# A planner that prices transfers by their packets, and a last tile whose sums lie in two places of PSUM

## The chip, the cores and the metric

The kernel runs on one core of a Trainium2 chip. The metric is device time in microseconds (us) of one execution. TensorE is called PE, its weight load PEld, VectorE DVE, ScalarE ACT, GpSimd POOL and SyncE SP. A q behind an engine's name (SPq, ACTq) is its sequencer, which issues DMAs.

## What is computed

Block-causal attention over 8 batches of 8 heads (576 positions of width 64), and behind it a gated feed-forward layer over the 4608 tokens, all in float32:

```python
scores = scale * np.matmul(q, k.transpose(0, 1, 3, 2))
mask = block_i >= block_j                    # blocks of 64 positions
scores = np.where(mask, scores, -1000000000.0)
attn = np.exp(scores - np.max(scores, axis=-1, keepdims=True))
attn = attn / (np.sum(attn, axis=-1, keepdims=True) + 1e-09)
x = np.matmul(attn, v)                       # (tokens, 512)
g = x @ w_gate                               # 512 x 1536
val = x @ w_val                              # 512 x 1536
out = (g * (1.0 / (1.0 + np.exp(-g))) * val) @ w_out     # 1536 x 512
```

q, k and v are float32; the three weights arrive as float64 words and are made float32 on the chip.

## The kernel before, in words

**Feed-forward.** The 4608 tokens are cut into 18 tiles of 256. A tile walks through the 12 chunks of 128 hidden columns two at a time (`feed_forward`): 24 matmuls against the gate's weights into a PSUM tile `gv` (lines 969 to 971), 24 against the value's weights into the other, then on ACT and DVE the tanh (L1002), two products (L1005, L1010), and the result split into a high and a low part `hhl` (cast L1015 on ACT, subtraction L1018 on DVE). From `hhl` and the weights of the output the down products (L1060 to L1062) go into the sums `po`, a PSUM tile of [128, 2, 512]: two blocks of 128 tokens, m = 0 and 1. Each product is made of three matmuls: high times high, high times low, low times high. After the last pair of chunks the sums are copied to SBUF by ACT (L1080) and stored by SP (L1084), one copy and one store for each m.

**Weights.** There are 36 pieces (12 chunks, of gate, value and output). Each is loaded as 512 KB into one of five slots `wo` (L822), made float32 by two steps of ACT (L837, L841) and two of DVE (L846, L851), and split into high (ACT L856) and low (DVE L859). Parts of the output's weights are written to `wo_d` in HBM (L875, L878) and fetched again by every later tile (L1035).

**Attention.** Batches 0 and 1 are "early": their queries come in stretches of 256 and 320, q and k are loaded in blocks of 96 rows (L359), turned on PE (L383), copied by ACT (L391), multiplied (L409), evacuated (L427, L432, L450, L453), reduced to a maximum (DVE L583, POOL L587), subtracted (DVE L611), put through exp (ACT L615) and multiplied with v (L655, v loaded by L632 and L637). Their PSUM tiles are `at` (two) and, for early batches, also `po`. Later batches load q and k by L482 and multiply at L535.

**What sets the order.** Every operation is a task with an engine, a cost in us, a rank, what it comes after, and the buffers it uses. The function `in_order` plays the engines through time: a free engine takes the ready task of the lowest rank whose buffers have room. For a transfer it keeps one clock, `queue`: the transfer occupies all of it for `t.moves`, and lands 0.9 us later:

```python
if t.moves:
    queue = max(queue, end + 0.65) + t.moves
    done = queue + 0.9
```

The resulting list is the order in which each engine's instructions stand in the program. On the chip each engine works through its own list in order and waits at each instruction for what it needs; there is no second choice. SP's list is nearly all of the DMA issues, and a transfer also waits for the one that used the same of eight semaphores, eight transfers earlier.

In `dma` (lines 155 to 159) `t.moves` is the size over 360 KB per us, whatever the transfer's shape; several calls give a round size (3e5 for a v load or an x store).

Of the kernel before, what the change touches and what calls it, by code (L numbers as in the profile page):

```python
# [18 lines left out]
def kernel(  # L19
# [17 lines left out]
    nc = tc.nc  # L37
    B, H, S, D = q.shape
    NT, DM = out.shape
    DFF = w_gate.shape[1]  # L40
    P = 128
# [4 lines left out]
    SP = NKC * P  # L46
# [11 lines left out]

    FINE = 4

    PATIENCE = 10.0
# [5 lines left out]
    TILES = [XT] * (NT // XT)  # L67
# [74 lines left out]
    def act_us(n):  # L142
        return 0.08 + n * 0.000833
# [10 lines left out]

    def dma(rank, size, fn, after=(), bufs=(), n=1, engine="SP"):

        t = add(engine, 0.5 * n, rank, fn, after, bufs)
        t.moves = size / 3.6e5
        return t
# [121 lines left out]
    for i in range(7):  # L281
        n = 2**i
# [31 lines left out]
    def attention(R, b, h, a, e, early, bufs, lane):  # L314
# [9 lines left out]
        W = e - a  # L324
# [25 lines left out]
        def plain_scores():  # L350
# [4 lines left out]
            def load_qk(i, queue):  # L355
# [9 lines left out]
            ld = [  # L365
                dma(R, 5e4 * len(blocks[1]), lambda: load_qk(0, nc.sync), [], [qk], 2),
                dma(R, 5e4 * len(blocks[1]), lambda: load_qk(1, nc.scalar), [], [qk], 2, "ACT")
                if early and a == b == 0
                else dma(R, 5e4 * len(blocks[1]), lambda: load_qk(1, nc.sync), [], [qk], 2),
            ]  # L370
# [97 lines left out]
        def split_scores():  # L468
# [19 lines left out]
            for i in range(2):  # L488
# [15 lines left out]

                ld = dma(R, 3e5, lambda i=i: load(i), [], [raw], 4)
                tr = add("DVE", dve_us(S), R, turn, [ld], [raw, turned, high, *prt])
# [134 lines left out]

        vl = dma(R, 3e5, load_v, [], [vt], 3 if e % P else 2)
        segs = [s for s in ((0, 2 * P), (2 * P, S)) if a <= s[0] and s[1] <= e]
# [124 lines left out]

        t = dma(R, 3e5, x_out, ends, [xu])
        x_done.extend((b, hd, a + here, e, t) for hd in heads)  # L770
# [21 lines left out]
    def weight(i, kind):  # L792
# [30 lines left out]

        t = chain["w"] = dma(R, 5e5, load, [chain["w"]], [raw])
        bufs = [raw, wo] if wo else [raw]
# [44 lines left out]
        if kind == 2:  # L870
            w_kept[i] = t, wo, part

            def store():
                if wo:
                    nc.sync.dma_start(out=wo_d[i], in_=wo[0].bitcast(F32))  # L875
                    return
                for j in range(2):
                    nc.sync.dma_start(  # L878
                        out=wo_d[i][:, j].rearrange("p (n m) -> p n m", n=parts), in_=part(j).bitcast(F32)
                    )  # L880

            t = dma(R, 5e5, store, [t], [wo] if wo else [], 2 if away else 1)
            if away:
                before_place.append((t, away))
# [59 lines left out]
    def feed_forward(j, t0, w, xs):  # L944

        E = 0.5 + j / 1000.0
        nb = w // P
        acc = Buf("po", also=("at",) if j == 1 else ())
        ends = [None] * nb
# [36 lines left out]
        for i in range(0, NFC, 2):  # L986
# [65 lines left out]
            for piece in pieces:  # L1052

                def products(i=i, piece=piece, hh=hh, took=took):
                    for y, m in piece:
                        whi, wlo = (took[y][2](k) for k in range(2))
                        bs = slice(y * w + m * P, y * w + (m + 1) * P)
                        po = acc[0][:, m].rearrange("p (n m) -> p n m", n=whi.shape[1])
                        hi, lo = hh[0][:, bs], hh[1][:, bs]
# [5 lines left out]
                after = [a, *(took[y][0] for y in ys), *{ends[m] for m in ms}]  # L1065
                bufs = [acc, hh, *(took[y][1] for y in ys if took[y][1])]
                t = add("PE", mm_us(DM, DM, DM) * len(piece), rank(i), products, after, bufs)
# [8 lines left out]
        for m in range(nb):  # L1076
            ob = Buf("ob", "out")

            def out_of_psum(m=m, ob=ob):
                nc.scalar.copy(ob[0], acc[0][:, m])  # L1080

            def store(m=m, ob=ob):
                r0 = t0 + m * P
                nc.sync.dma_start(out=out[r0 : r0 + P, :], in_=ob[0])  # L1084

            e = add("ACT", act_us(DM), E, out_of_psum, [ends[m]], [acc, ob])
            dma(E, 2.6e5, store, [e], [ob])

# [184 lines left out]
```

## Time and profile before

| | |
|---|---|
| three runs | 1189.08, 1189.09, 1189.10 us; median 1189.09 |
| the profiled execution | 1189.82 us |
| its span, first to last instruction | 1188.0 us |
| PE busy | 1152.1 us, 97% of the span |
| DVE, ACT, POOL busy | 760.3, 638.0, 325.7 us |
| DMA | 197.39 MB, 166 GB/s over the span |
| mean granted TensorE clock | 0.996 of full speed |

How to read it: busy time is the union of an engine's instructions. The page has the span in 40 slices, each engine's busy share in tenths. A window's line gives the length of a stretch, then for PE, PEld, DVE, ACT and POOL the busy us and the number of instructions, the mean granted clock, the DMA engines' busy share and GB/s. A line of the timeline is: start, duration, engine, source line, operation, written tile <- read tiles, shape, how many in a row, and in brackets the idle time before it and what ended it. A line of the chain (the work that ended last, followed back) has start, duration and what.

### The profile page before, as it was taken

The numbers are of one execution on the slowest core, as the hardware profiler recorded it, in microseconds if no ns is written. First come the engines' busy times: TensorE is split into PE (matmuls) and PEld (weight loads), VectorE is DVE, ScalarE is ACT, GpSimd is POOL, SyncE is SP. The second block draws the span as 40 slices with busy tenths as digits, with TensorE's granted clock in tenths as the row PEclk, the third lists the DMA queues.
The fourth block names the chain that finished last, engine by engine and source line by source line (L and its number), as shares of the span: only waits on it lengthen the run. The fifth ranks groups of instructions, "written<-read, shape, count | busy, mean of one in ns | idle before, by whom it ended". The sixth has DMA issues, their size and how long they took to land.

```text
span 1188.0 us, 21711 instructions
## 1 busy us (share of the span) xinstructions
PE 1152.1 (97%) x8464; PEld 1030.1 (87%) x8464; DVE 760.3 (64%) x1233; ACT 638.0 (54%) x1150; POOL 325.7 (27%) x138
## 2 busy tenths in 40 slices
PE   6789999999999999999999999999999999999998
PEld 4557777898889899989898989898989899999997
DVE  5889879766678585957686768576767533323222
ACT  5879957756566655556565555474736312212111
POOL 3121211033444433324342525243253400000000
PEclk9899999999999999999999999999999999999999
DMA  7857765675556656665656456555652455444442
GB/s 184 231 160 212 211 176 173 174 216 141 145 159 179 177 145 158 178 194 159 174 168 184 149 155 165 185 147 183 165 179 99 157 162 171 155 169 135 142 133 98
DMA packets 266838, 197.39 MB, mean 166 GB/s; under 512 B 195248, under 2 KB 231104, under 8 KB 266736
## 3 DMA queue, kind: packets, MB, share of 16 engines
q1 hardware_dynamic: 264304, 195.42, 56.5%
q8 instruction: 66, 1.08, 0.4%
q10 hardware_dynamic: 2432, 0.59, 0.2%
q14 instruction: 36, 0.29, 0.1%
HBM read 171.57 MB, written 24.38 MB: 165 GB/s over the span
## 4 chain that ended last, share of the span: by engine, by line
PE 85%; DVE 5%; ACT 5%; DMA 3%; issue 1%; POOL 0%; SPq 0%; ACTq 0%; POOLq 0%
PE gv L969 15%; PE gv L971 15%; PE gv L970 15%; PE po L1060 8%; PE at L655 8%; PE po L1061 8%; PE po L1062 8%; PE at L535 7%; DMA wo<-in_moe_w_gate_dram 1%; DVE sc L611 1%; DMA wo<-in_moe_w_val_dram 1%; PE at L409 1%; ACT ob L837 1%; ACT qk L497 1%; DVE mx L583 1%
## 5 line engine op out<-in xcount | busy, mean ns | idle before, releaser
L587 POOL PARTITION_ALL_REDUCE mx<-mx x80 | 144.7, 1855 | 397.4 <-DVE mx L583 155.8
L971 PE MATMUL gv<-xhl,v_all 128*128 128x256 f32 x864 | 239.6, 277 | 1.9 <-DVE v_all L859 1.9
L969 PE MATMUL gv<-xhl,v_all 128*128 128x256 f32 x864 | 241.1, 279 | 0.2 <-DVE t L1005 0.2
L706 POOL PARTITION_ALL_REDUCE mx<-mx x48 | 178.7, 3770 | 224.1 <-DVE mx L583 192.0
L970 PE MATMUL gv<-xhl,v_all 128*128 128x256 f32 x864 | 239.4, 277 | 0.0
L1005 DVE SCALAR_TENSOR_TENSOR t<-t,gv 128x512 f32<-128x512 f32 x108 | 73.8, 684 | 200.0 <-ACT t L1002 199.7
L969 PEld LDWEIGHTS gv<-xhl,v_all 128*128 128x128 f32 x864 | 162.2, 188 | 3.7 <-issue 1.9
L971 PEld LDWEIGHTS gv<-xhl,v_all 128*128 128x128 f32 x864 | 162.3, 188 | 2.1 <-DVE v_all L859 2.1
L970 PEld LDWEIGHTS gv<-xhl,v_all 128*128 128x128 f32 x864 | 162.3, 188 | 0.9
L1060 PE MATMUL po<-wo,hhl 128*128 128x512 f32 x396 | 157.0, 396 | 1.6 <-ACT ob L1080 1.6
L1061 PE MATMUL po<-wo,hhl 128*128 128x512 f32 x396 | 154.9, 391 | 0.0
L1062 PE MATMUL po<-wo,hhl 128*128 128x512 f32 x396 | 154.4, 390 | 0.0
L1002 ACT ACTIVATE t<-gv 128x512 f32<-128x512 f32 x108 | 64.7, 599 | 158.4 <-PE gv L971 158.0
L1015 ACT CAST hhl<-t 128x512 fp32r<-128x512 f32 x108 | 67.0, 621 | 129.7 <-DVE t L1010 125.2
L611 DVE TENSOR_TENSOR sc<-sc,mx 128x640 f32<-128x640 f32 (+6 forms) x168 | 122.5, 768 | 15.5 <-POOL mx L587 15.2
L1018 DVE TENSOR_TENSOR hhl<-t,hhl 128x512 fp32r<-128x512 f32 x108 | 94.6, 876 | 49.2 <-ACT hhl L1015 48.5
L615 ACT ACTIVATE sc<-sc 128x1024 f32<-128x1024 f32 (+3 forms) x104 | 105.5, 1030 | 37.5 <-DVE sc L611 36.4
L969 PE MATMUL gv<-xhl,g_even 128*128 128x256 f32 x432 | 123.4, 286 | 1.3 <-DVE t L1005 1.2
L971 PE MATMUL gv<-xhl,g_even 128*128 128x256 f32 x432 | 122.2, 283 | 0.2 <-DVE g_even L859 0.2
L970 PE MATMUL gv<-xhl,g_even 128*128 128x256 f32 x432 | 122.1, 283 | 0.0
L969 PE MATMUL gv<-xhl,g_odd 128*128 128x256 f32 x432 | 121.1, 280 | 0.0
L970 PE MATMUL gv<-xhl,g_odd 128*128 128x256 f32 x432 | 119.6, 277 | 0.0
(154 smaller groups left out, 2411.6 us busy)
## 6 DMA issues: line engine op xcount, KB each, us to landing
wo<-wo_d SPq DMA_DIRECT2D x200, 512.0 KB
out_dram<-ob SPq DMA_DIRECT2D x36, 256.0 KB
v<-in_v_dram SPq DMA_DIRECT2D x64, 128.0 KB
xt<-x_d SPq DMA_DIRECT2D x64, 128.0 KB
rt<-r_d SPq DMA_DIRECT2D x128, 64.0 KB
qk<-in_q_dram SPq DMA_DIRECT2D x112, 72.0 KB
qk<-in_k_dram SPq DMA_DIRECT2D x104, 72.0 KB
x_d<-xu SPq DMA_DIRECT2D x24, 288.0 KB
```

Of the source, the lines that this page charges most:

```text
L587: nc.gpsimd.partition_all_reduce(m, m, channels=P, reduce_op=bass_isa.ReduceOp.max)
L611: nc.vector.tensor_tensor(piece(c), scores_of(c), m, ALU.subtract)
L615: nc.scalar.activation(x, x, AF.Exp)
L655: nc.tensor.matmul(ps[0][own(x), 1 - i if sums else i, q0 - s0 : s1 - s0], lhsT=ones if sums else vt[0][:, 2 * lane + c, own(x)], rhs=sc[0 ...
L706: nc.gpsimd.partition_all_reduce(m, m, channels=P, reduce_op=bass_isa.ReduceOp.add)
L969: nc.tensor.matmul(o, lhsT=hi[:, d], rhs=xhi[:, 0:w], start=first, stop=False)
L970: nc.tensor.matmul(o, lhsT=hi[:, d], rhs=xlo[:, 0:w], start=False, stop=False)
L971: nc.tensor.matmul(o, lhsT=lo[:, d], rhs=xhi[:, 0:w], start=False, stop=last)
L1018: nc.vector.tensor_tensor(hh[1][:, 0:n], t[0][:, 0:n], hh[0][:, 0:n].bitcast(F32), ALU.subtract)
L1060: nc.tensor.matmul(po, lhsT=hi, rhs=whi, start=i + y == 0, stop=False)
L1061: nc.tensor.matmul(po, lhsT=hi, rhs=wlo, start=False, stop=False)
L1062: nc.tensor.matmul(po, lhsT=lo, rhs=whi, start=False, stop=i + y == NFC - 1)
```

## The change

Three things are changed. The planner's transfers get a length from their packet size (the contiguous bytes of one piece): a packet of n bytes takes 9 + 0.0385 n ns on one of 16 DMA engines. So a megabyte takes 2.95 us in the planner's eyes at 1024 bytes (the default), 4.60 at 256, 6.80 at 128 and 2.54 at 4096, where it was 2.78 for all. The sizes of some loads are put right at the same time (v, x, the first q blocks). `AHEAD` is empty and `LATER` is 0.0, so what they are put into is unchanged.

```diff
-    def dma(rank, size, fn, after=(), bufs=(), n=1, engine="SP"):
+    def dma(rank, size, fn, after=(), bufs=(), n=1, engine="SP", packet=1024):
 
         t = add(engine, 0.5 * n, rank, fn, after, bufs)
-        t.moves = size / 3.6e5
+        t.moves = size / packet * (9.0 + 0.0385 * packet) / 16e3
         return t
...
-                dma(R, 5e4 * len(blocks[1]), lambda: load_qk(0, nc.sync), [], [qk], 2),
-                dma(R, 5e4 * len(blocks[1]), lambda: load_qk(1, nc.scalar), [], [qk], 2, "ACT")
+                dma(R, 5e4 * len(blocks[0]), lambda: load_qk(0, nc.sync), [], [qk], 2, packet=256),
+                dma(R, 5e4 * len(blocks[1]), lambda: load_qk(1, nc.scalar), [], [qk], 2, "ACT", 256)
...
-                ld = dma(R, 3e5, lambda i=i: load(i), [], [raw], 4)
+                ld = dma(R, 3e5, lambda i=i: load(i), [], [raw], 4, packet=128)
...
-        vl = dma(R, 3e5, load_v, [], [vt], 3 if e % P else 2)
+        vl = dma(R + (LATER if early else 0.0), 512.0 * e, load_v, [], [vt], 3 if e % P else 2, packet=256)
...
-        t = dma(R, 3e5, x_out, ends, [xu])
+        t = dma(R, 512.0 * (W - here), x_out, ends, [xu])
...
-        t = chain["w"] = dma(R, 5e5, load, [chain["w"]], [raw])
+        t = chain["w"] = dma(AHEAD.get((i, kind), R), 5e5, load, [chain["w"]], [raw], packet=1024 if kind < 2 else 4096)
...
-            t = dma(R, 5e5, store, [t], [wo] if wo else [], 2 if away else 1)
+            t = dma(R, 5e5, store, [t], [wo] if wo else [], 2 if away else 1, packet=512 if away else 4096)
```

In the last tile the sums of the two token blocks lie in two PSUM tiles of the kind `at`, and the second block's copy is made in halves of 256 columns, one by ACT and one by DVE, each half with a store of its own, the second one issued by ACT:

```diff
-        acc = Buf("po", also=("at",) if j == 1 else ())
+        ends_alone = j == len(TILES) - 1
+        if ends_alone:
+            accs = [Buf("at") for _ in range(nb)]
+        else:
+            accs = [Buf("po", also=("at",) if j == 1 else ())] * nb
...
+            halves = 2 if ends_alone and m == nb - 1 else 1
+            for x in range(halves):
+                cols = slice(x * DM // halves, (x + 1) * DM // halves)
+                def out_of_psum(m=m, ob=ob, x=x, cols=cols):
+                    if x:
+                        nc.vector.tensor_copy(ob[0][:, cols], sums(m)[:, cols])
+                    else:
+                        nc.scalar.copy(ob[0][:, cols], sums(m)[:, cols])
...
+                e = add("DVE" if x else "ACT", us, E, out_of_psum, [ends[m]], [accs[m], ob])
+                dma(E, 2.6e5 / halves, store, [e], [ob], engine="ACT" if x else "SP")
```

Because the planner's clock differs, the order differs on every engine from the first transposes on, with the same operations. On SP the last difference ahead of the end stands near row 500 of 690. Three places matter below. (The line numbers of the changed kernel are higher: 3 up to L862, 12 in the feed-forward, 19 at the last copy.)

The first is on SP, where the gate's and the value's third pieces (slots `wo1`, `wo2`) are issued among the loads of q and k (`qk0`, `qk1`), of v (`v1`) and two stores to `wo_d`. Before:

```order
L822 DMA wo0_0_94<-in_moe_w_out_dram 128x1024
L878 DMA wo_d_120<-g_even0_76 128x4x128
L878 DMA wo_d_120<-g_even1_77 128x4x128
L359 DMA qk1_0_143<-in_q_dram 96x4x64 x2
L359 DMA qk1_0_143<-in_k_dram 96x6x64 x2
L822 DMA wo1_0_95<-in_moe_w_gate_dram 128x4x256
L359 DMA qk0_0_123<-in_q_dram 96x3x64 x2
L359 DMA qk0_0_123<-in_k_dram 96x3x64 x2
L359 DMA qk0_0_123<-in_q_dram 96x3x64 x2
L359 DMA qk0_0_123<-in_k_dram 96x3x64 x2
L822 DMA wo2_0_96<-in_moe_w_val_dram 128x4x256
```

and now:

```order
L825 DMA wo0_0_94<-in_moe_w_out_dram 128x1024
L881 DMA wo_d_120<-g_even0_76 128x4x128
L881 DMA wo_d_120<-g_even1_77 128x4x128
L635 DMA v1_0_154<-in_v_dram 128x4x64 x2
L640 DMA v1_0_154<-in_v_dram 64x2x64
L825 DMA wo1_0_95<-in_moe_w_gate_dram 128x4x256
L362 DMA qk1_0_139<-in_q_dram 96x4x64 x2
L362 DMA qk1_0_139<-in_k_dram 96x6x64 x2
L362 DMA qk0_0_123<-in_q_dram 96x3x64 x2
L362 DMA qk0_0_123<-in_k_dram 96x3x64 x2
L825 DMA wo2_0_96<-in_moe_w_val_dram 128x4x256
L362 DMA qk0_0_123<-in_q_dram 96x3x64 x2
```

The load of `v1` has moved behind the stores (it stood ahead of them), the gate ahead of two pairs of `qk1`, and the value's piece ahead of two pairs of `qk0`; between gate and value lie eight transfers in both.

The second is on DVE, at the first subtractions of the early attention's second round; `v_all1` is the low part of the value's weights. Before:

```order
L306 TENSOR_TENSOR xhl5_1_89<-xt1_0_299,xhl5_0_88 128x256
L846 SCALAR_TENSOR_TENSOR wo1_0_95<-wo1_0_95,ob1_0_278 128x512
L611 TENSOR_TENSOR sc0_0_220<-sc0_0_220,mx0_0_181 128x2x320
L1005 SCALAR_TENSOR_TENSOR t1_0_750<-t1_0_750,gv0_0_139 128x512
L611 TENSOR_TENSOR sc0_0_220<-sc0_0_220,mx0_0_181 128x2x192
L611 TENSOR_TENSOR sc0_0_220<-sc0_0_220,mx0_0_181 128x2x320
L611 TENSOR_TENSOR sc0_0_220<-sc0_0_220,mx0_0_181 128x2x64
L611 TENSOR_TENSOR sc0_0_220<-sc0_0_220,mx0_0_181 128x2x320
L583 TENSOR_TENSOR mx1_0_231<-sc1_0_282 128x2x320
L859 TENSOR_TENSOR v_all1_74<-wo0_0_94,v_all0_73 128x4x128
```

and now:

```order
L1017 SCALAR_TENSOR_TENSOR t1_0_729<-t1_0_729,gv0_0_142 128x512
L309 TENSOR_TENSOR xhl5_1_89<-xt1_0_296,xhl5_0_88 128x256
L862 TENSOR_TENSOR v_all1_74<-wo0_0_94,v_all0_73 128x4x128
L614 TENSOR_TENSOR sc0_0_223<-sc0_0_223,mx0_0_184 128x2x320
L614 TENSOR_TENSOR sc0_0_223<-sc0_0_223,mx0_0_184 128x2x192
L614 TENSOR_TENSOR sc0_0_223<-sc0_0_223,mx0_0_184 128x2x320
L614 TENSOR_TENSOR sc0_0_223<-sc0_0_223,mx0_0_184 128x2x64
L614 TENSOR_TENSOR sc0_0_223<-sc0_0_223,mx0_0_184 128x2x320
```

The low part of the weights has moved from behind the five subtractions and a maximum to ahead of them.

The third is the end of ACT's list, the last tile's copies, here with the semaphores that each row waits for (PE, DVE or Activation for an engine's, DMAHW for a transfer's). Before:

```order
L1015 CAST hhl0_0_99<-t0_0_486 128x512 [waits DVE_49]
L1002 ACTIVATE t1_0_750<-gv1_0_146 128x512 [waits PE_49,Activation_49]
L1015 CAST hhl1_0_101<-t1_0_750 128x512 [waits DVE_49]
L1080 COPY ob0_0_2184<-po0_0_214 128x512 [waits DMAHW5_49,PE_49]
L1080 COPY ob1_0_2199<-po0_0_214 128x512 [waits DMAHW7_49]
```

and now:

```order
L1014 ACTIVATE t1_0_729<-gv1_0_148 128x512 [waits PE_49,Activation_49]
L1027 CAST hhl1_0_101<-t1_0_729 128x512 [waits DVE_49]
L1099 COPY ob0_0_2140<-at0_0_168 128x512 [waits DMAHW5_49,PE_49]
L1099 COPY ob1_0_2151<-at1_0_187 128x256 [waits DMAHW7_49,DVE_49]
L1103 DMA out_0_dram<-ob1_0_2151 128x256 [waits DMAHW1_49]
```

ACT's half of the second copy waits for DVE; DVE's half (`COPY ob1_0_2151<-at1_0_187 128x256`, its last row) waits for PE. ACT issues the store of DVE's half behind its own half.

## Rows read from the trace of the kernel before

**Rows 1.** The page: busy time of PE, and the span in 40 slices.
```profile
PE 1152.1 (97%) x8464; PEld 1030.1 (87%) x8464; DVE 760.3 (64%) x1233; ACT 638.0 (54%) x1150; POOL 325.7 (27%) x138
...
PE   6789999999999999999999999999999999999998
```

**Rows 2.** Busy time by window: the start by tens, all of 0 to 300, a steady stretch.
```profile
20.00:30.00 10.00, 6.73 (x62) 4.98 (x60) 9.62 (x26) 7.68 (x14) 2.29 (x3) 1.00 0.58 163
30.00:40.00 10.00, 8.26 (x76) 6.19 (x72) 9.76 (x20) 10.00 (x21) 0.00 (x0) 1.00 0.90 233
40.00:50.00 10.00, 6.91 (x56) 5.67 (x52) 9.73 (x17) 7.53 (x16) 2.87 (x2) 1.00 0.90 228
50.00:60.00 10.00, 7.29 (x33) 3.79 (x35) 6.38 (x8) 8.43 (x12) 2.76 (x2) 0.66 0.81 231
...
80.00:90.00 10.00, 8.15 (x60) 5.18 (x58) 7.34 (x14) 7.00 (x13) 3.97 (x2) 0.83 0.57 163
...
0.00:300.00 300.00, 270.14 (x1946) 218.44 (x1947) 231.07 (x422) 220.55 (x406) 71.77 (x52) 0.98 0.67 188
...
500.00:600.00 100.00, 100.00 (x739) 90.54 (x738) 68.60 (x107) 59.57 (x106) 36.92 (x14) 1.00 0.61 175
```

**Rows 3.** Timeline, 46 to 53 us: PE, DVE and ACT around the first down product.
```profile
46.96 0.28 PE L971 MATMUL gv<-xhl,v_all 128*128 128x256 f32 x1
...
47.42 0.68 DVE L1010 SCALAR_TENSOR_TENSOR t<-t,gv 128x512 f32<-128x512 f32 x1
...
49.75 0.77 ACT L837 ACTIVATE ob<-wo 128x512 f16<-128x512 f32 x1 [2.47 <-DMA wo<-in_moe_w_val_dram]
...
52.05 0.60 ACT L1015 CAST hhl<-t 128x512 fp32r<-128x512 f32 x1
...
52.71 0.80 PE L1060 MATMUL po<-g_even,hhl 128*128 128x512 f32 x1 [5.47 <-ACT hhl L1015]
```

**Rows 4.** The chain of waits, 38 to 50 us: two weight loads from issue to landing.
```profile
38.48 6.12 DMA wo<-in_moe_w_gate_dram
...
44.61 0.31 SPq L359
...
44.97 4.76 DMA wo<-in_moe_w_val_dram
```

**Rows 5.** Timeline: the same 20 matmuls with v, at two clocks.
```profile
54.29 4.32 PE L655 MATMUL at<-sc,v 128*64 128x320 f32 x20
...
66.20 2.27 PE L655 MATMUL at<-sc,v 128*64 128x320 f32 x20
```

**Rows 6.** Timeline, 77 to 87 us: the value's weights on ACT, DVE and PE.
```profile
77.42 0.70 ACT L856 CAST v_all<-wo 128x512 fp32r<-128x512 f32 x1
...
81.78 0.69 DVE L859 TENSOR_TENSOR v_all<-wo,v_all 128x512 fp32r<-128x512 f32 x1
...
82.53 0.39 PE L971 MATMUL gv<-xhl,v_all 128*128 128x256 f32 x1 [1.85 <-DVE v_all L859]
...
83.42 3.67 PE L655 MATMUL at<-sc,v 128*64 128x320 f32 x20
```

**Rows 7.** Chain and timeline at the end: last matmuls of each block, copies, stores.
```profile
1182.02 0.23 PE po L1062
...
1183.38 0.24 PE po L1062
...
1183.65 1.07 ACT L1080 COPY ob<-po 128x512 f32<-128x512 f32 x2 [4.12 <-PE po L1062]
1184.26 0.83 SPq L1084 DMA_DIRECT2D out_dram<-ob  x2
```

**Rows 8.** DMA view of 1182 to 1190 us, GB/s in 40 slices of 0.2 us.
```profile
GB/s 0 0 0 0 0 0 0 0 0 0 0 0 0 0 0 184 389 420 379 440 379 399 31 0 0 0 0 0 0 0 0 0 0 0 41 0 0 0 0 0
```

**Rows 9.** Groups by line: copies and sums that read 256 columns of PSUM.
```profile
L670 ACT COPY xu<-at 128x256 f32<-128x256 f32 (+2 forms) x60 | 20.8, 388 | 52.1 <-PE at L655 49.9 <-DVE sr L682 1.9
...
L689 DVE TENSOR_TENSOR xt<-at,xt 128x256 f32<-128x256 f32 x6 | 2.5, 420 | 0.5 <-ACT parts L391 0.5
```

**Rows 10.** Waits of SP's queue, the longest.
```profile
SPq L1035 <- PE po L1062: 262.9, 60, 11.2
```

More of the change, by code (lines that the diff above doesn't have):

```diff
@@ L59 @@
     FINE = 4
+    AHEAD = {}
+    LATER = 0.0
     PATIENCE = 10.0
@@ L365, in plain_scores @@
             ld = [
-                dma(R, 5e4 * len(blocks[1]), lambda: load_qk(0, nc.sync), [], [qk], 2),
-                dma(R, 5e4 * len(blocks[1]), lambda: load_qk(1, nc.scalar), [], [qk], 2, "ACT")
+                dma(R, 5e4 * len(blocks[0]), lambda: load_qk(0, nc.sync), [], [qk], 2, packet=256),
+                dma(R, 5e4 * len(blocks[1]), lambda: load_qk(1, nc.scalar), [], [qk], 2, "ACT", 256)
                 if early and a == b == 0
-                else dma(R, 5e4 * len(blocks[1]), lambda: load_qk(1, nc.sync), [], [qk], 2),
+                else dma(R, 5e4 * len(blocks[1]), lambda: load_qk(1, nc.sync), [], [qk], 2, packet=256),
             ]
@@ L947, in feed_forward, with sums @@
         nb = w // P
-        acc = Buf("po", also=("at",) if j == 1 else ())
+        ends_alone = j == len(TILES) - 1
[3 more added lines that the diff above has]
+            accs = [Buf("po", also=("at",) if j == 1 else ())] * nb
+        def sums(m):
+            return accs[m][0][:, 0 if ends_alone else m]
         ends = [None] * nb
@@ L1057, in products @@
                         bs = slice(y * w + m * P, y * w + (m + 1) * P)
-                        po = acc[0][:, m].rearrange("p (n m) -> p n m", n=whi.shape[1])
+                        po = sums(m).rearrange("p (n m) -> p n m", n=whi.shape[1])
                         hi, lo = hh[0][:, bs], hh[1][:, bs]
@@ L1065, in feed_forward @@
                 after = [a, *(took[y][0] for y in ys), *{ends[m] for m in ms}]
-                bufs = [acc, hh, *(took[y][1] for y in ys if took[y][1])]
+                bufs = [*dict.fromkeys(accs[m] for _, m in piece), hh, *(took[y][1] for y in ys if took[y][1])]
                 t = add("PE", mm_us(DM, DM, DM) * len(piece), rank(i), products, after, bufs)
@@ L1077, in feed_forward, with store @@
             ob = Buf("ob", "out")
[L1079 to L1087, printed above, removed]
+            halves = 2 if ends_alone and m == nb - 1 else 1
[6 more added lines that the diff above has]
+                        nc.scalar.copy(ob[0][:, cols], sums(m)[:, cols])
+                def store(m=m, ob=ob, x=x, cols=cols):
+                    r0 = t0 + m * P
+                    (nc.scalar if x else nc.sync).dma_start(out=out[r0 : r0 + P, cols], in_=ob[0][:, cols])
+                us = (dve_us if x else act_us)(DM // halves)
+                e = add("DVE" if x else "ACT", us, E, out_of_psum, [ends[m]], [accs[m], ob])
+                dma(E, 2.6e5 / halves, store, [e], [ob], engine="ACT" if x else "SP")
     at_work = []
```

## The prediction

> **What bounds the kernel now.** I read the page first: PE is busy 97% of the span, and its 40 slices are at 9 everywhere but in the first four and the last [rows 1]. So only PE's idle time and slow clock can be won, and I looked for where they lie. The windows say: from 500 to 600 us PE is busy 100.00 of 100 us; from 0 to 300 us it is busy 270.14, which leaves 29.9 us, 10.8 of it between 20 and 60 us [rows 2], and by the page's slices nearly all before 120 us. There the other engines are nearly full as well: DVE is busy 9.6 to 9.8 of each 10 us from 20 to 50 us, ACT 10.00 from 30 to 40. Two windows show a lower granted clock, 50 to 60 us (mean 0.66) and 80 to 90 us (0.83) [rows 2]. The same 20 matmuls with v took 4.32 us in the first and 2.27 us at 66.20 [rows 5], so these are spells at 1.2 instead of 2.4 GHz. A mean of 0.66 over 10 us is 6.8 us at 1.2 GHz, at most 3.4 us lost; 0.83 is 3.4 us and at most 1.7 us lost. Both spells come behind a stall of PE.
>
> The timeline shows the two stalls. At 52.71 PE starts the first down product (L1060) after 5.47 us, released by ACT's cast L1015 [rows 3]. DVE had the cast's operand ready at 48.10 (L1010, 47.42 and 0.68), so ACT was late: it had stood 2.47 us at L837 for a piece of the value's weights, and worked through what lies between [rows 3]. That piece landed at 49.73, after 4.76 us; the gate's piece ahead of it took 6.12 us, and the value's could be issued only behind the SP row that the gate's landing released at 44.61 [rows 4]. At 82.53 PE had waited 1.85 us for the low part of the value's weights, which DVE (L859) made at 81.78 though ACT's high part started at 77.42 [rows 6]. The end is the third place: the last matmul of block m = 0 ends at 1182.25, that of m = 1 at 1183.62, and both copies start behind the latter [rows 7].
>
> **What the planner's lengths change.** By the formula and the sizes in the diff, a first q transfer costs the planner 0.69 us instead of 0.42, a q or k block 1.38 or 2.04 instead of 0.83, a v load of 512 positions 1.21, a gate or value piece 1.48 instead of 1.39, an output piece 1.27. No instruction is added or removed by it; rows change places. After 300 us I cost this at nothing: PE is full, and SP's commonest long wait there is for PE (60 issues, 262.9 us in all [rows 10]), so transfers are issued as soon as PE frees a buffer. If that cover is gone at one place, the price is one load's landing, 4.76 to 6.12 us [rows 4]. What is left is the start and the tail.
>
> **Term 1, the tail: -0.5 us.** Now both copies, 1.07 us together, follow the last matmul, since both sums are one tile [rows 7]. In the changed kernel m = 0 has a tile of its own: its copy and store can run from 1182.25, beside m = 1's last matmuls, and leave the path. For m = 1 the order shows ACT's half waiting for a DVE row, so I take the halves one behind the other: 0.42 and 0.39 us for 256 columns [rows 9] and some 0.03 between, from 1183.65 to 1184.49 instead of 1184.72. That gains 0.23. Then 256 KB instead of 512 KB lie behind the last issue: at the 379 to 440 GB/s shown, 0.65 instead of 1.3 us [rows 8]; but the old first store was issued at 1184.26, so part of the 0.65 was over before. Data flowed till about 1186.45; issued about 0.25 earlier with half the bytes it ends near 1185.95. Bounds: -0.2 (only the copies' gain) and -0.95 (halves side by side, one issue on each queue).
>
> Here a row and a rule can be weighed. The order shows a semaphore of DVE at ACT's half, and no row of before has two engines reading one PSUM tile at once, so rows alone leave -0.5 and -0.9 open. The Trainium skill, "PSUM — Partial Sum Buffer", section "PSUM bank collisions raise a hardware error", says that two engines must not touch the same bank and the same 32 partitions at the same time, reads included, and that the compiler's scheduler makes such instructions wait for each other. By that rule splitting the copy speaks against itself: two halves of 0.42 and 0.39 us in turn are longer than the whole copy, about 0.54 (half of 1.07), and only the separate tiles would gain; the term stays -0.5. Without it, it would be -0.9. No run so far shows which.
>
> **Term 2, the first down product: -1.6 us.** On SP the gate's piece moves ahead of two q and k pairs of `qk1`, and the value's piece ahead of two pairs of `qk0`: two runs of 147 KB, 295 KB less in front of it. At 228 to 233 GB/s [rows 2] that is 1.28 us. What made the value's piece late (the semaphore shared with the gate's, eight transfers earlier) is unchanged, but the gate's is issued behind 295 KB of `v1` instead of 491 KB of `qk1`, some 0.8 us sooner. ACT's wait at L837 was 2.47 us: that is the most that an earlier landing can give, and then ACT is next, since its list in front of the cast has the same work in both orders. I take -1.6, above the 1.28 and below the cap; bounds 0 and -2.47. Moved with it: `v1` now stands behind two stores, and waits for PE's product that frees its buffer; gate and `qk1` queue behind it. That is rival C.
>
> **Term 3, the value's weights: -0.8 us.** On DVE the low part moves ahead of five subtractions and a maximum. PE's wait was 1.85 us [rows 6]; with DVE free the high part (77.42 plus 0.70) would set it, but the matmul stands where PE's other work has put it by then, and the subtractions it overtakes are late instead: exp and the products with v wait for them. So part comes back; I take a little under half, with bounds 0 and -1.85.
>
> **Sum.** -0.5 - 1.6 - 0.8 = -2.9 against the profiled execution, 1189.82 us (1188.0 of span and 1.82 outside): 1186.9. The profiled execution lies 0.73 above the median of the three runs, 1189.09, so against the median 1186.2, or -0.24%. A measurement of this kernel can tell 0.2%, 2.4 us, from no change: faster is below 1186.7, slower above 1191.5. The forecast alone lies close to that edge. Its own range, terms at their bounds, is 1189.09 - 0.2 = 1188.9 to 1189.09 - 0.95 - 2.47 - 1.85 = 1183.8.
>
> **Rivals.**
>
> A, the tail only: the stalls move but their sum stays, as DVE and ACT are nearly full from 20 to 50 us [rows 2] and a load or a low part made earlier only pushes back something else. For: 9.7 of 10 us busy on DVE leaves no room for gains from order alone. Against: ACT stood idle 2.47 us for a transfer [rows 3], which is no shortage of ACT. Time: 1189.09 - 0.5 = 1188.6.
>
> B, stalls and slow clock gone: if PE's pauses at 52.71 and 82.53 become short, the clock stays at 2.4 GHz. Term 1 and the caps: -0.5 - 2.47 - 3.4 - 1.85 - 1.7 = -9.9, so 1179.2. For: both spells follow a stall [rows 2, 3, 6], and are half of the price. Against: both stalls must go at once, and of the 5.47 us at most 3.95 can (the cast may start at 48.10 at the earliest [rows 3]).
>
> C, slower: `v1`'s load, now behind the stores, holds SP until PE has done the product that still reads its buffer, and this product now waits for a PSUM tile that ACT must empty. Gate, `qk1` and the value's piece stand behind it in SP's list. Price: one load's landing, 4.76 us [rows 4], less the 1.28 us of bytes taken out: 3.5 us, and with the tail 1189.09 + 3.5 - 0.5 = 1192.1. It decides when the value's piece lands after 49.73, so that the first down product starts after 52.71. For: SP works in order, and ACT is busy 10.00 of 10 us from 30 to 40 us [rows 2], just where that tile must be emptied. Against: the two stores that were ahead of these loads before wait for DVE and PE too, so part of the wait was there already.
>
> That the change does not do what it says is possible for the halves (they run in turn), and is in term 1.
>
> **Chances.** The forecast 0.40, of which 0.33 below 1186.7 and 0.07 within 0.2%; A 0.22, all within 0.2%; B 0.15, faster; C 0.23, slower. Faster 0.48, same 0.29, slower 0.23. The range goes from 1179.0, just under B, to 1192.5, a little over C: half of C's cases, where more than one load is late, and few of B's lie outside. The forecast's own range is 1183.8 to 1188.9.
>
> **What the new profile would show.** Term 1: m = 0's copy starts before the last matmul, and ACT's half behind DVE's; data ends some 2.3 us after the last matmul instead of 2.8. If the halves start together, -0.9 was right. Term 2: ACT's wait for the value's piece shrinks from 2.47 to about 0.9 us and PE starts the first down product near 51.1; the window of 50 to 60 us has a clock above 0.66. Term 3: the wait for `v_all` before the value's matmul is under 1.1 us. Right in B: clock 1.00 in both windows. Right in C: a wait of SP at `v1`'s load for PE, and the first down product after 52.71. The forecast is wrong as a whole if PE's idle time before 300 us, 29.9 us now, does not shrink, or if new idle time of PE stands after 300 us.

## The result, and the profile after

The changed kernel takes 1193.05 us in the median (1190.78 to 1197.72, 9 runs), the kernel before 1188.67 us (1187.96 to 1190.31, 9 runs). The ratio is 1.0035, with a 95% interval of 1.0023 to 1.0047: **slower by 0.35%**, 4.4 us, where 1186.2 was forecast, and above the range's end of 1192.5. The profiled execution took 1193.95 us, with a span of 1191.3 us.

The windows of the changed kernel, with the columns of [rows 2], say where the time went. Long windows that weren't shown of the kernel before come first:

```profile
0.00:360.00 360.00, 328.53 (x2381) 271.62 (x2382) 273.96 (x486) 257.58 (x472) 95.85 (x60) 0.99 0.65 180
360.00:390.00 30.00, 30.00 (x227) 27.52 (x227) 25.91 (x45) 17.40 (x30) 12.65 (x4) 1.00 0.67 180
390.00:1180.00 790.00, 790.00 (x5845) 728.31 (x5842) 460.20 (x704) 361.97 (x648) 217.16 (x74) 1.00 0.54 160
```

The same windows of the changed kernel:

```profile
0.00:360.00 360.00, 332.37 (x2400) 274.62 (x2401) 278.75 (x488) 258.61 (x473) 95.13 (x60) 0.99 0.65 182
360.00:390.00 30.00, 26.23 (x172) 23.89 (x171) 24.03 (x41) 15.36 (x26) 11.78 (x4) 0.89 0.61 173
390.00:1180.00 790.00, 790.00 (x5855) 727.61 (x5854) 460.87 (x704) 361.71 (x649) 217.31 (x74) 1.00 0.53 160
```

Up to 360 us PE idles 27.6 us instead of 31.5, so the start did get better. Behind 390 us both are full to the last hundredth. Between them, in a stretch where the kernel before has no idle time at all, the changed one idles 3.77 us and has a mean clock of 0.89: 6.6 of 30 us at 1.2 GHz, worth 3.3 us. The stretch costs some 7.1 us, by a clock that is given to two digits.

The stall itself, on PE's timeline of the changed kernel (columns as in [rows 3]). These are the down products of the last pair of chunks of the fourth tile of tokens (tile 3, from 0):

```profile
358.57 0.40 PE L1072 MATMUL po<-wo,hhl 128*128 128x512 f32 x1
...
362.97 0.28 PE L983 MATMUL gv<-xhl,v_all 128*128 128x256 f32 x1
365.50 0.50 PE L1072 MATMUL po<-wo,hhl 128*128 128x512 f32 x1 [2.26 <-ACT hhl L1027]
...
367.75 0.79 PE L1074 MATMUL po<-wo,hhl 128*128 128x512 f32 x1 [1.52 <-DVE hhl L1030]
368.34 0.63 PE L1072 MATMUL po<-wo,hhl 128*128 128x512 f32 x1
...
372.18 0.41 PE L981 MATMUL gv<-xhl,g_even 128*128 128x256 f32 x1
```

PE ends the value's products at 363.2 and has the down products next in its list; they need `hhl`, which DVE and ACT can only make from those very products. The same matmul took 0.40 us at 358.57 and 0.63 at 368.34: the half clock. In the kernel before, 48 products of the next tile (24 gate, 24 value, from 365.89 to 371.40 us) stand between the two. On PE's timeline of the kernel before:

```profile
365.77 0.28 PE L971 MATMUL gv<-xhl,v_all 128*128 128x256 f32 x1
365.89 0.28 PE L969 MATMUL gv<-xhl,g_even 128*128 128x256 f32 x1
...
371.28 0.28 PE L971 MATMUL gv<-xhl,v_all 128*128 128x256 f32 x1
371.40 0.40 PE L1060 MATMUL po<-wo,hhl 128*128 128x512 f32 x1
```

PE's order shows it, counted by kind (V value, G gate, D down products), before and then now; all D here are tile 3's, G and the V behind them the next tile's:

```
V9   G24  V24  D9   G24  V24  D3   G24
V12  D12  G24  V24
```

DVE and POOL in the same stretch of the changed kernel:

```profile
357.69 0.69 DVE L1030 TENSOR_TENSOR hhl<-t,hhl 128x512 fp32r<-128x512 f32 x1
...
363.11 1.09 DVE L586 TENSOR_TENSOR mx<-sc 128x896 f32<-128x896 f32 x1
364.11 0.69 DVE L1022 SCALAR_TENSOR_TENSOR t<-t,gv 128x512 f32<-128x512 f32 x1
364.71 1.44 DVE L496 STREAM_TRANSPOSE sr<-qk 128x576 f32<-128x576 f32 x2
366.07 1.63 DVE L1030 TENSOR_TENSOR hhl<-t,hhl 128x512 fp32r<-128x512 f32 x1
367.62 0.75 DVE L309 TENSOR_TENSOR xhl<-xt,xhl 128x256 fp32r<-128x256 f32 x2
```
```profile
363.36 4.61 POOL L590 PARTITION_ALL_REDUCE mx<-mx  x2 [10.42 <-ACT xhl L306]
```

The low parts of the next tile's input (L309) are behind all of that, and end at 368.4: the 48 products could not have filled the hole as DVE's list stands.

The places of [rows 3, 6] in the changed kernel, ACT first, then PE:

```profile
48.56 0.79 ACT L840 ACTIVATE ob<-wo 128x512 f16<-128x512 f32 x1
...
50.89 0.60 ACT L1027 CAST hhl<-t 128x512 fp32r<-128x512 f32 x1
```
```profile
51.55 0.50 PE L1072 MATMUL po<-g_even,hhl 128*128 128x512 f32 x1 [2.47 <-ACT hhl L1027]
...
81.66 2.28 PE L658 MATMUL at<-sc,v 128*64 128x320 f32 x20 [3.45 <-ACT parts L394]
```

ACT no longer waits for the value's piece, and PE's wait for the first down product fell from 5.47 to 2.47 us. The wait for `v_all` is gone, and 3.45 us in front of a product with v are new.

The tail, which answers to [rows 7], the last matmul of the kernel before first, then the changed kernel:

```profile
1183.22 0.39 PE L1062 MATMUL po<-wo,hhl 128*128 128x512 f32 x1
```
```profile
1186.39 0.59 ACT L1099 COPY ob<-at 128x512 f32<-128x512 f32 x1 [2.76 <-PE at L1074]
...
1187.32 0.39 PE L1074 MATMUL at<-wo,hhl 128*128 128x512 f32 x1
1187.75 0.42 DVE L1097 COPY ob<-at 128x256 f32<-128x256 f32 x1 [3.40 <-PE at L1074]
1188.21 0.37 ACT L1099 COPY ob<-at 128x256 f32<-128x256 f32 x1 [1.23 <-DVE ob L1097]
```

The first block's copy runs before the last matmul, the halves one behind the other. The last matmul begins at 1187.32 instead of 1183.22 us, 4.10 later. That is a late loss less an early lead, and both can be read from the lines above: the value's last product of tile 3 starts at 362.97 instead of 365.77 us, a lead of 2.80; from there to the last matmul (the late part, below) it is 824.35 instead of 817.45 us, 6.90 more. From the start of the last matmul to the end of the span it is 3.99 instead of 4.73 us. 4.10 - 0.74 is the growth of the span, from 1188.0 to 1191.3 us.

### The profile page after: what moved, and what is told of

Read it like the earlier page. It is cut to its first block, busy times and chain, and to the rows that moved or that the text cites. A ratio compares the mean times of both kernels' runs of the same rounds, so it can differ in the third digit from the quotient of the medians.

```text
span 1191.3 us, 21716 instructions
## 1 busy us (share of the span) xinstructions
PE 1156.3 (97%) x8464; PEld 1032.5 (87%) x8464; DVE 766.1 (64%) x1234; ACT 637.5 (54%) x1150; POOL 324.2 (27%) x138
## 4 chain that ended last, share of the span: by engine, by line
PE 69%; DVE 1%; DMA 0%; SPq 0%; issue 0%; ACT 0%; DVEq 0%
PE gv L981 13%; PE gv L983 13%; PE gv L982 13%; PE po L1072 6%; PE po L1074 6%; PE po L1073 6%; PE at L538 5%; PE at L658 5%; PE at L1073 0%; PE at L1072 0%; PE at L1074 0%; DVE sc L614 0%; DMA xt<-x_d 0%; DVE hhl L1030 0%; DVE xt L938 0%; DVE mx L586 0%
## 5 line engine op out<-in xcount | busy, mean ns | idle before, releaser
L1072 PE MATMUL po<-wo,hhl 128*128 128x512 f32 x372 | 148.2, 398 | 2.3 <-ACT hhl L1027 2.3
L1074 PE MATMUL po<-wo,hhl 128*128 128x512 f32 x372 | 146.1, 393 | 1.5 <-DVE hhl L1030 1.5
L1073 PE MATMUL po<-wo,hhl 128*128 128x512 f32 x372 | 146.3, 393 | 0.0
L548 ACT ACTIVATE sc<-at 128x576 f32<-128x576 f32 x96 | 80.3, 838 | 77.1 <-PE at L538 73.7
L981 PE MATMUL gv<-xhl,g_odd 128*128 128x256 f32 x432 | 120.8, 280 | 0.0
L1030 DVE TENSOR_TENSOR hhl<-t,hhl 128x512 fp32r<-128x512 f32 x108 | 94.4, 874 | 39.6 <-ACT hhl L1027 38.8
```

Source lines behind the costliest of these rows:

```text
L548: nc.scalar.mul(sc[0][:, x, o : o + 2 * gw].rearrange("p (i n) -> p i n", i=2), ps[0][:, :, 0:gw], SCALE)
L981: nc.tensor.matmul(o, lhsT=hi[:, d], rhs=xhi[:, 0:w], start=first, stop=False)
L1030: nc.vector.tensor_tensor(hh[1][:, 0:n], t[0][:, 0:n], hh[0][:, 0:n].bitcast(F32), ALU.subtract)
L1072: nc.tensor.matmul(po, lhsT=hi, rhs=whi, start=i + y == 0, stop=False)
L1073: nc.tensor.matmul(po, lhsT=hi, rhs=wlo, start=False, stop=False)
L1074: nc.tensor.matmul(po, lhsT=lo, rhs=whi, start=False, stop=i + y == NFC - 1)
```

## The experiments

Each comparison is with runs of the kernel before on the same chip; that median lay between 1188.7 and 1191.9 us from chip to chip, so ratios are given.

**The changed kernel again**, for a second and a third profile.

> The changed kernel once more, unaltered, for a second profile. Theory (order of PE at the end of the fourth token tile): the stall of about 3.8 us near 365 us and the half-clock spell behind it are there again, since PE's list is fixed; the first 355 us are again some 2 to 4 us ahead of the kernel before. Rival (chance: a late transfer in that one execution): no stall near 365 us, and the time 3 to 7 us shorter than 1193.95.

> The changed kernel unaltered, timed on the same chip as the kernel with all edits. Theory: 1192 to 1195 us, slower than before by 3 to 5 us, as in the first comparison. Rival (that was one chip's state): within 1 us of before.

1194.4 us in the one execution; in the second comparison 1193.45 us (10 runs), ratio 1.0026 (1.0011 to 1.0040). Both profiles have the stall, 2.06 and 1.52 us, then 2.19 and 1.52 us, and a mean clock of 0.94 from 360 to 390 us; the late part is 823.06 and 823.37 us. It belongs to the order. The lead was not there again as expected: the value's last product of tile 3 starts at 364.90 and 365.12 us, only 0.9 and 0.65 ahead of the kernel before.

**A cover for nine of the twelve down products.**

```diff
-                if j >= FINE:
+                if j >= FINE or j == FINE - 1 and i == NFC - 2 and piece != pieces[0]:
                     chain["down"].append(t)
```

> The changed kernel, with nine of the twelve down products that end the fourth tile put behind the next tile's 48 products on PE, as they stand in the kernel before. Theory (missing cover): the stall of 2.26 and 1.52 us and the spell at half clock near 365 us go, 7.0 us in all, and the kernel is at 1185 to 1187 us, faster than before by 2 to 4 us. Rival (the inputs of the next tile are late in themselves): PE waits for them instead, the stall only moves by a few us, and the time stays at 1191 to 1194. Second rival (clock alone): idle goes but another spell at half clock comes, 1188 to 1190.

1192.52 us, ratio 1.0033 (1.0020 to 1.0046). The theory's number fell: PE waited 2.41 and 1.51 us as before, since the first three of the twelve, which I had left in place, are the ones that wait. The edit was too small to decide between the theories.

**The stall put into the kernel before.**

```diff
+                if j == FINE - 1 and i == NFC - 2:
+                    bare.append(t)
...
-                        [ts, *(xs[d][0] for d in ds), w_done[i + y, which]],
+                        [ts, *(bare if j == FINE and i == 0 else []), *(xs[d][0] for d in ds), w_done[i + y, which]],
```

> The kernel before, with the next tile's products held back at that one place, so that all twelve down products stand right behind the value products as in the changed kernel. Theory (missing cover): PE idles 2 to 4 us there and falls to half clock, so the kernel is slower by 4 to 7 us: 1193 to 1196. Rival (the stall needs the changed kernel's late inputs or its lead of 2.8 us): less than 1.5 us slower.

1196.65 us, ratio 1.0061 (1.0046 to 1.0077), some 7 us. PE's line and the window of 360 to 390 us:

```profile
369.19 0.80 PE L1062 MATMUL po<-wo,hhl 128*128 128x512 f32 x1 [3.06 <-ACT hhl L1017]
```
```profile
360.00:390.00 30.00, 26.67 (x168) 23.79 (x167) 24.90 (x40) 16.59 (x28) 12.65 (x4) 0.89 0.61 173
```

3.33 us idle and again 6.6 us at half clock, 6.6 us lost in all (the late part is 824.26 us): this one place, with nothing else of the change, costs what the changed kernel loses there. It needs no lead: the value's last product stands at 365.85 us, as in the kernel before.

**The last tile alone**, with the old lengths, twice; and a version of it without halves.

```diff
-        t.moves = size / packet * (9.0 + 0.0385 * packet) / 16e3
+        t.moves = size / 3.6e5
```
```diff
-            halves = 2 if ends_alone and m == nb - 1 else 1
+            halves = 1
```

> The kernel before with the last tile's change alone (two PSUM tiles, halves), the lengths as before. Theory: all of the order up to the last tile is as before, the stretch from the end of the last matmul to the end of the span falls from 4.4 to about 3.6 us, and the time by 0.8: 1187.9 to 1188.3, no difference that the timing can tell. Rival (the tail does more or less than that, as the halves run one after the other): 0 or over 1.5 us.

> The last tile's change alone once more, on the same chip: 0.5 to 1.5 us under the kernel before.

> The kernel before with two PSUM tiles in the last tile, but the second block's copy whole on ACT and one store on SP, so without halves. Theory (separate tiles give the gain, halves in turn cost what they save): from the start of the last matmul to the end of the span 3.9 to 4.2 us, as with halves (3.98 to 4.16) and against 4.73 before. Rival (halves and two queues matter): 4.4 us or more. Rival (halves in turn cost): under 3.85.

1187.86 us, ratio 0.9999 (0.9989 to 1.0009), and 1188.99 us, ratio 0.9992 (0.9982 to 1.0003): no difference that timing can tell. In the traces the stretch from the start of the last matmul to the end of the span is 4.73 us in the kernel before (5.25 in the run with the stall put in), with separate tiles and halves 3.98 to 4.00 in the changed kernel and its variants and 4.16 or 4.17 in six profiles of the kernel before with the changed last tile, and 4.03 with separate tiles and a whole copy in the latter, one profile:

```profile
1183.38 0.58 ACT L1099 COPY ob<-at 128x512 f32<-128x512 f32 x1 [0.77 <-PE at L1074]
```

So the separate tiles give the gain, 0.56 to 0.75 us, and the halves nothing: next to the six profiles the whole copy is 0.13 us shorter.

**PE's list alone, then DVE's too, then ACT's, then more**: the changed kernel's finished order with single rows moved at the end of tile 3. `move(t, u)` puts task t just ahead of u in the list, and `mark` holds the tasks of that place by name: `next` the 48 products, `down` the twelve, `low` the low parts of the next tile's input.

```diff
     order = in_order()
+    for t in (*mark["low"][2:], *mark["next"]):
+        move(t, mark["down"][0])
```

> The changed kernel with one edit of PE's list and of no other: the next tile's 48 products (gate and value of its first pair) ahead of all twelve down products that end the fourth tile. Theory A (PE's order alone: the twelve need the cover): the stall of 3.8 us and the half clock near 365 us go, 1185 to 1187 us. Theory B (the low parts of the next tile's input are late too, since DVE's list has them behind the last pair's work: they ended near 368.4 us, and PE could have begun them at 363.3): PE idles 4 to 5 us there all the same, in front of the gate's products, 1191 to 1194 us.

1198.55 us, ratio 1.0077 (1.0058 to 1.0096), worse than either theory said. PE now waits in front of the gate's products, and once more later:

```profile
368.99 0.58 PE L984 MATMUL gv<-xhl,g_even 128*128 128x256 f32 x1 [3.77 <-DVE xhl L309]
...
381.63 0.39 PE L983 MATMUL gv<-xhl,g_even 128*128 128x256 f32 x1 [3.33 <-DVE t L1022]
```

Theory B's wait is there, 3.77 us for L309; its time was 4 us too low for the second wait, which neither foresaw. PE's order alone is not the cause.

```diff
+    for t in (*mark["low"][2:], dve[last - 5]):
+        move(t, dve[last - 4])
```

> The same edit of PE's list, and on DVE the two last low parts of the next tile's input moved ahead of two maxima, the last pair's product, two transposes and a subtraction. Theory B: the low parts end near 364.2 us, PE idles about 1 us there instead of 3.8, the clock stays at 2.4 GHz, and the kernel is at 1185 to 1188 us. Theory A: no better than the edit of PE alone. Rival (the reduction on POOL then blocks DVE's other work): idle time of 2 us or more remains in front of the down products, 1189 to 1192.

1192.6 us, ratio 1.0015 (1.0003 to 1.0027). The first stall is gone, the one in front of the following pair stays, since ACT's tanh for it stands behind the copies of the old sums:

```profile
374.84 0.58 PE L983 MATMUL gv<-xhl,g_even 128*128 128x256 f32 x1 [3.46 <-DVE t L1022]
```

```diff
+    move(mark["tanh"], act[act.index(mark["out"]) - 1])
+    move(mark["silu"], dve[dve.index(mark["silu"]) - 3])
```

> The edits of PE's and DVE's lists at the end of the fourth tile, and one more on ACT and DVE: the next tile's tanh moved ahead of an exp and of the two copies of the old sums, and its first product ahead of three rows of attention. Theory (the place is one knot of three lists: each edit moved the wait to the engine that still had the old order): the idle time of 3.46 us near 375 us and the half clock there go, no stall over 1.2 us stands after 250 us, and the kernel is at 1185 to 1188 us, faster than before. Rival (the work does not fit: DVE and ACT are short of time there, so that a wait of over 2 us comes up a fourth time): 1189 to 1193.

1190.29 us, ratio 1.0010 (0.9999 to 1.0020): most of the loss is back, but not the forecast, and the rival was right that a wait comes up again:

```profile
375.25 0.41 PE L983 MATMUL gv<-xhl,v_all 128*128 128x256 f32 x1 [1.99 <-DVE t L1027]
```

```diff
+    move(mark["gated"], divide)
+    move(mark["high"], act[act.index(mark["high"]) - 1])
+    order.remove(divide)
+    order.insert(order.index(mark["low0"]) + 1, divide)
```

> The edits so far, and two more: on DVE the multiply of a later tile's input moved behind the next tile's second product and its subtraction, on ACT the cast of that product ahead of the cast of that input. Theory (the wait moved a third time, to DVE's product of the next tile, which stood behind a row that waited 1.18 us for a transfer and then took 1.60 us beside a reduction on POOL): the idle time of 1.99 us near 375 us and the spell behind it go, and the time is 1186 to 1188.5 us, 1.5 to 3 us less than with three edits. Rival (a further wait in the same stretch takes its place): over 1.5 us of idle time between 362 and 390 us, and 1189 to 1191.

1191.83 us, ratio 1.0010 (0.9997 to 1.0022): no better. That wait went, and PE waited 2.87 us at 384.12 instead. The place is a knot of three lists that belong together; freeing one row makes the next one late.

**The old length for the later q and k loads alone.**

```diff
                 ld = dma(R, 3e5, lambda i=i: load(i), [], [raw], 4, packet=128)
+                ld.moves = 3e5 / 3.6e5
```

> The changed kernel, with the old length (0.83 us in the planner) for the loads of q and k of the later batches, and the new one for all else. Theory (these loads, 2.04 us each in the planner, are what shifted the late stretch): the place at the fourth tile's end is as in the kernel before, no stall near 365 us, and 1185 to 1189 us. Rival (any change of the early order shifts it): another stall of 2 us or more stands after 150 us, 1190 to 1195.

1193.22 us, ratio 1.0039 (1.0027 to 1.0051). The order at tile 3's end is as in the kernel before, and the wait near 365 us is down to 1.06 us, but 1.07 and 1.53 us for a piece of `wo` (at 203.65 and 243.82) and 1.40 us at 520.57 are new. The rival holds in substance (its 2 us were not reached): it is not one length; another clock gives another order, with its own stalls.

**The early order of the changed kernel joined to the late order of the kernel before** (`OLD` is the list of task numbers in that order, `TURN` the planner's time of the join, 180 and 130 us).

```diff
+                cand = [
+                    t for t in rest[e][:1] if now > TURN and t in could[e] and t.ready <= now
+                ] if now > TURN else sorted(
```

> The changed kernel's order as long as the planner's clock is under 180 us, and from there on every engine takes its remaining tasks in the order of the kernel before; the last tile as changed. Theory (the loss is all in the late order that the new lengths gave, the gain all in the early one and the tail): no stall over 1.6 us after 250 us, the lead of 2 to 5 us over the kernel before that the changed kernel has at 150 us stays to the end, and the time is 1184 to 1187 us, faster than both. Rival (the lead itself makes the stall, since PE comes early to inputs that are not there): a stall of 2 us or more between 300 and 400 us again, 1188 to 1193.

> The same, joined at 130 us of the planner's clock. Theory: 1184 to 1187 us as well, nearer to the lower end, since the changed kernel's lead is largest near 140 us. Rival: as with the later join, 1188 to 1193.

1193.54 us, ratio 1.0011 (0.9999 to 1.0023), and 1192.95 us, ratio 1.0014 (1.0002 to 1.0025). Behind 250 us no stall is over 1.63 us, and that one the kernel before has too (1.60). But the seam made stalls of its own (2.40 us at 201.16; 1.92, 1.30 and 2.17 us between 144 and 153), so the lead was gone when the place came, and both forecasts of the time missed. The late part settles the rest: it is 817.48 and 817.44 us here, behind the changed early order, and 817.43 to 817.48 in all ten profiles with the late order of the kernel before, against 823.06 to 824.35 in the three of the changed kernel. So the whole loss is in the late order. A lead does survive the place with the old one: in the profile of the loads alone (below) the value's last product of tile 3 starts at 363.04 us, 2.7 ahead of the kernel before, and the late part is 817.45.

**One early term at a time**, on the kernel before with the changed last tile: a row of DVE, two rows of SP, both, and the two rows again, timed. The numbers are tasks: 1884 the low part, 184 the first of the subtractions, 1849 and 1856 the gate's and the value's piece, 202 and 265 the first of the loads that they pass.

```diff
+    move(1884, 184)
```
```diff
+    move(1849, 202)
+    move(1856, 265)
```

> The kernel before with the changed last tile, and one row of DVE moved: the low part of the value's weights ahead of the five subtractions and the maximum. Forecast (third term): the wait in front of the value's matmul, 1.60 to 1.87 us in the four profiles of that order so far, falls under 1.1 us, and about 0.8 us of it stays won at 100 us. Rival (it all comes back through the late subtractions): the wait goes and a new one of 1.5 us or more stands in front of a product with v within 10 us.

> The same kernel with two rows of SP moved: the gate's piece ahead of two loads of qk1, the value's piece ahead of two loads of qk0, as in the changed kernel, and nothing else. Forecast (second term): the wait in front of the first down product, 4.1 to 5.5 us in the profiles of that order, falls by 1.6 us. Rival (the value's piece still waits for the gate's landing, and what is moved back is late instead): a fall of under 0.5 us, or a new wait in front of the transposes of qk1 or qk0.

> Both moves in one kernel, with the changed last tile. If both terms hold: faster than before by 2 to 4 us (0.2 to 0.3%) and faster than the last tile's change alone by 1.5 to 3 us. Rival (DVE and ACT are full, the stalls only move): no different from the last tile's change alone.

> The last tile's change and the two moved rows of SP alone, now timed. The second term and the tail hold without the low part's move: 1.5 to 2.5 us under the kernel before (0.13 to 0.21%). Rival (spells at half clock eat it, as one near 140 us did in the single look): under 0.1%.

The control (the last tile alone, on the same chip), the low part moved, and the loads moved:

```profile
52.45 0.80 PE L1072 MATMUL po<-g_even,hhl 128*128 128x512 f32 x1 [4.87 <-ACT hhl L1027]
...
81.90 0.58 PE L983 MATMUL gv<-xhl,v_all 128*128 128x256 f32 x1 [1.69 <-DVE v_all L862]
```
```profile
83.18 0.80 PE L658 MATMUL at<-sc,v 128*64 128x320 f32 x2 [2.13 <-ACT parts L394]
```
```profile
51.11 0.78 PE L1072 MATMUL po<-g_even,hhl 128*128 128x512 f32 x1 [3.40 <-ACT hhl L1027]
```

With the low part moved, the wait of 1.69 us is gone and 2.13 us stand 1.3 us later: the rival's number. DVE's line says why, here behind the control's row in the same place:

```profile
76.94 0.83 DVE L614 TENSOR_TENSOR sc<-sc,mx 128x640 f32<-128x640 f32 x1 [1.14 <-POOL mx L590]
```
```profile
77.89 0.69 DVE L862 TENSOR_TENSOR v_all<-wo,v_all 128x512 fp32r<-128x512 f32 x1 [1.71 <-ACT v_all L859]
```

The row now stands in front and waits 1.71 us for ACT's high part, with the subtractions behind it; in the control the first of them had to wait there too, but 1.14 us and for POOL. With the loads moved, the wait for the first down product falls by 1.47 us, and ACT's wait for the value's piece from 2.00 to 0.36, on ACT's timeline of the control and of the loads moved:

```profile
49.49 0.78 ACT L840 ACTIVATE ob<-wo 128x512 f16<-128x512 f32 x1 [2.00 <-DMA wo<-in_moe_w_val_dram]
```
```profile
48.12 0.78 ACT L840 ACTIVATE ob<-wo 128x512 f16<-128x512 f32 x1 [0.36 <-DMA wo<-in_moe_w_val_dram]
```

PE's wait is 2.62 to 3.40 us in the three profiles with the loads moved, and 4.12 to 5.47 in the six with the old rows. How much of it stays won is less sure: the value's last product of tile 3 starts at 363.04, 364.86 and 365.29 us in those three, and at 364.17 to 365.85 in five with the old early order.

In time: the low part moved 1189.90 us and the loads moved 1188.67 in one execution each; both moves 1188.28 us (12 runs), ratio 0.9986 (0.9974 to 0.9998), which is 0.7 us under the last tile's change alone on that chip, less than forecast and not clear of noise, as the rival had it; the loads alone 1187.47 us (1184.73 to 1191.51, 12 runs), ratio 0.9979 (0.9965 to 0.9992). The last tile's change with these two rows of SP is **faster than both kernels**, by 0.21% against the one before. What the two rows add to the last tile's change, whose own ratios were 0.9999 and 0.9992, the timings don't separate: the intervals overlap.

## Why the prediction was wrong

**Term 1, the tail: right.** -0.74 us in the changed kernel and -0.56 with the last tile alone, for -0.5. The halves ran in turn, DVE at 1187.75 and ACT at 1188.21, and -0.9 was not reached. This agrees with the rule of the Trainium skill that was weighed ("PSUM — Partial Sum Buffer", "PSUM bank collisions raise a hardware error"); no run here had both engines read one PSUM tile at once. That the separate tiles alone give the gain is shown by the run without halves.

**Term 2, the loads: the mechanism is right, its worth in time only partly shown.** -1.6 forecast, -1.47 in PE's wait with the two rows alone; in the changed kernel ACT's wait is gone, and the first down product starts at 51.55 (51.1 was said), 1.16 earlier.

**Term 3, the low part: wrong.** "I take a little under half" of the 1.85 us; nothing stays. The text named what would be late, but gave the row no wait of its own. Moved up, it waits for ACT, and everything behind it on DVE waits with it.

**"After 300 us I cost this at nothing": the step that failed.** The ground was that SP's loads wait for PE there, so order could not matter. In the changed kernel that holds for loads (behind 300 us no wait of PE over 1 us ended with a transfer), and from 390 us on for all. The text did ask what a lost cover would cost, but only the cover of a load. Yet PE is full at 365 us in the kernel before only because 48 products stand between the last value products and the down products that hang on them, and that cover is a matter of the order of PE, ACT and DVE, not of transfers. The new order takes it away: 3.77 us idle and 3.3 us lost to half clock, 6.90 us in the late part. The places examined beforehand were those where the trace of before has stalls; the change made one where it has none. The prediction's own sign for being wrong as a whole, new idle time of PE after 300 us, is what came; the other one did not, as the idle time before 300 us shrank from 29.9 to 27.35 us. One reading was off without consequence: the page's slices are under 9 in the first three, not four.

**The rivals.** C's time, 1192.1, was near, for a reason that did not happen: the first down product came earlier, not after 52.71, and SP waited for PE at `v1` for 0.6 us at most, not for a load's landing. A and B are out; the clock from 50 to 60 us rose only to 0.83.

**Sum.** In the profiled pair a lead of 2.8 us for the early terms' 2.4, the tail's 0.74 for 0.5, and 6.9 us against them that stood at nothing. That the lead fits so well is in part luck. In eight profiles with the changed early order the value's last product of tile 3 starts at 360.71 to 365.12 us (mean 363.2), in five with the old one at 364.17 to 365.85 (mean 365.1): 1.9 us on average, with a spread as large as the term.

## What to carry to other kernels

When a planner's costs change, compare the finished order of the engine that bounds over its whole length, above all where the trace of before shows it full: look for each product that hangs on the one just ahead of it, and whether what stood between them still does. Another cost model in a list scheduler draws a new order, and its value is what that order happens to hide (whether the new lengths are nearer to the transfers' true ones was not measured here); the last tile and the two moved rows of SP are worth more alone (0.9979) than with the order that came with them (1.0035). And a row moved up in an in-order list needs its own inputs priced first.

## What the runs showed of the hardware

- DVE's subtraction L1030 took 0.69 us at 357.69 and 1.63 us at 366.07, while two reductions on POOL ran from 363.36 to 367.97. In the kernel before, 72 of these subtractions had no reduction beside them and took 0.63 to 0.69 us; of the 36 that had, 19 took 0.97 to 3.07 us, and 18 of these ended 0.27 to 0.52 us before the end of a reduction, whenever they had begun. The Trainium skill, "SBUF — State Buffer", "SBUF: two separate sides", says that a DVE instruction with two inputs in SBUF and a GpSimd one that reads SBUF take the same ports in turn, the later one waiting. The trace agrees. The kernel before has such a row at the same place too (1.45 us at 369.09), under the 48 products.
- PE fell to half clock behind the stalls of 1.99 us or more between 360 and 390 us in all nine profiles that have one (mean clock 0.89 or 0.94 in that window, so 6.6 or 3.6 us of it), but not behind the 3.45 us at 81.66 in the changed kernel's first profile (1.00 from 80 to 90 us), nor behind the 2.40 us at 201.16 in the run joined at 180 us (1.00 from 195 to 215 us). The same kernel's runs differ with it: of nine runs of the changed kernel the three with a mean clock of 0.994 took 1190.78 to 1192.35 us, the two with 0.993 1192.27 and 1193.95, the three with 0.991 took 1193.05 to 1194.88 and the one with 0.989 took 1197.72.
